# Softmax attention into a soft mixture of experts and a Mish block: the first head pair in an order of its own

## The chip, the cores and the metric

One core of a Trainium2 chip runs the whole program. The metric is device time in microseconds (us) of one execution; the kernel before takes 608.54 us (median of three runs, 608.24 to 610.33).

The engines are named as the profile names them: PE is TensorE (PEld its weight loads), DVE VectorE, ACT ScalarE, POOL GpSimd, SP the engine that issues nearly all DMA transfers. Each works through its own queue in order; a transfer is issued by one engine and carried out by the DMA engines.

## The reference

Three parts run one after the other: attention with rotary embeddings (4 batches, 8 heads, 576 positions, 64 per head), a soft mixture of experts, and a Mish block.

```python
def _attn_ref(q, k, v):
    ...
    def rotate(x):
        x1, x2 = (x[..., :half], x[..., half:])
        return np.concatenate([x1 * cos - x2 * sin, x1 * sin + x2 * cos], axis=-1)
    q_rot, k_rot = (rotate(q), rotate(k))
    scores = scale * np.matmul(q_rot, k_rot.transpose(0, 1, 3, 2))
    scores = scores - np.max(scores, axis=-1, keepdims=True)
    attn = np.exp(scores)
    attn = attn / (np.sum(attn, axis=-1, keepdims=True) + 1e-09)
    return np.matmul(attn, v)
```

The experts and the Mish block come after all the attention; the change touches nothing of them.

## The kernel before

The attention works through 16 pairs of heads. A pair's 576 positions are 512 main rows, loaded as four blocks of 128, and 64 rows that remain, loaded for all heads of a batch at once (`load_rem`).

For each pair, q and k are rotated (`rope_pair`, four tensor operations for each of q and k; `rope_rem` for the remaining rows), transposed on PE (`main_pe`, four transposes each; `rem_pe`, one), and split into a high part, rounded to the format fp32r, and the low part that is left (`main_hi` and `rem_hi` on ACT, `main_lo` and `rem_lo` on DVE, into the buffers `parth` and `partl`, one of each). The parts are then copied into stacks whose upper 64 partitions hold one part and whose lower 64 hold the other: `qk_st`, with k's high part above its low part, and `k2_st`, with the two exchanged, so that two products of 128 partitions give all four terms. For every pair but the first the copying is done by DMA (`stack_dma`, 12 transfers a pair); for the first pair before the change it is done by ACT and POOL (`stack_copy`), save two transfers.

Scores come in nine steps for each pair, S0 to S8 (`scores`): S0, S2, S4, S6 are the four row blocks of head 0, S1, S3, S5, S7 those of head 1, S8 the remaining rows of both. Each is a PSUM tile of two banks (pool `ps_s`, two of them); DVE takes the row maximum (M0 to M8, `maxima`), ACT the exponential with its sum (E0 to E8, `expo`). PE transposes the result (T0 to T7, K0, K1, R, Q), ACT or DVE copies it out (t0 to t7, k0, k1), and PE multiplies it with v (A0 to A4, B0 to B4), followed by x, Y, X and further small steps. All other PSUM tiles share the pool `ps_m` (four of one bank). In between, 20 pieces of later weights are converted from a wider format (`ci`, `Ca` on ACT, `Cb` on DVE, `Cs` on POOL, `co`).

The order of all this is one handwritten list, `PLAN`, gone through once for each pair (a period); `name@n` means that the step is done for the pair n periods back (negative: ahead), so G, ga, gd, Hk, hka, hkd, dk, Hq, hqa, hqd, dq feed the following pair. `keep_in_program_order` holds each engine to it. For the first period the tables `moved` and `shifted` put some steps elsewhere: the feeding of pair 1 begins at S4, pair 1's q is rotated on DVE (`ropeq1`, after M3), and two conversions are begun.

Ahead of the first period stands a prologue: constants and loads on SP, memsets, the rotation of the first k, of the remaining rows of two heads, and of the first q on DVE, the transposes with products of zeros between them (`busy(n)`, n products whose result nobody reads), and the split and the stacking.

Of the kernel before, what the change touches and what calls it, by code (L numbers as in the profile page):

```python
# [35 lines left out]


EVAC = {'t0': 'a', 't1': 'a', 't2': 'a', 't3': 'a', 't4': 'a', 't5': 'd', 't6': 'a', 't7': 'd', 'k0': 'a', 'k1': 'a'}


@with_exitstack
def kernel(
# [28 lines left out]
    psx = ExitStack()  # L71
    ps_s = psx.enter_context(tc.tile_pool(name="ps_s", bufs=2, space=PSUM))
    ps_m = psx.enter_context(tc.tile_pool(name="ps_m", bufs=4, space=PSUM))

# [135 lines left out]

    def load_pair(p, which="qk"):
        b, h = divmod(2 * p, H)
        for nm in which:
            src = q if nm == "q" else k
            t = work(2, 2 * "qk".index(nm) + p % 2, (2, 256))
            dma(out=t, in_=src[b, h:h + 2, 0:512, :].rearrange("h (p c) d -> p h (c d)", c=4))
            raw[nm, p] = t
# [9 lines left out]

    def load_rem(b):
        t = work(1, 3, (H, D))
        dma(out=t[0:R], in_=q[b, :, 512:S, :].rearrange("h s d -> s h d"))  # L230
        dma(out=t[R:128], in_=k[b, :, 512:S, :].rearrange("h s d -> s h d"))
        rem_raw[b] = t

# [42 lines left out]
    def parts_of_pair(p):  # L276
        for x in "hl":
            part[x, p] = ae.tile([128, 2, 640], F32R, tag="part" + x, name="part" + x)
# [21 lines left out]

    def main_part(p, nm, x):
        return part[x, p + 1][:, "qk".index(nm), R:R + 512]

# [79 lines left out]
    def out_of(on, dst, src):  # L383
        (act.copy if on == "a" else dve.tensor_copy)(dst, src)

    def t_copy(p, i):
        t, h = divmod(i, 2)
        tt = t % 2
        out_of(EVAC[f"t{i}"], pt_of(p, t // 2)[:, 5 * h:5 * h + 4, tt * 128:(tt + 1) * 128], m_ps.pop(("T", p, i)))

# [271 lines left out]

    nc.scalar.preload_act_table_set("exp_and_friends")
    pool_.memset(c_all, 0.0)
    dma(out=cs[:, C_COS:C_END], in_=cst[:, C_COS:C_END])
    load_pair(0, "k")
    dma(out=cs[:, 0:C_COS], in_=cst[:, 0:C_COS])
    load_rem(0)
    load_pair(0, "q")
    for i in range(2):  # L670
        dve.memset(qk_st[i][:, QZ:QAR].bitcast(F32), 0.0)
        dve.memset(vrem[i], 0.0)
        dve.memset(zs[i], 1e-9)
    dve.memset(st2, 1e-9)
    dve.memset(tmps[1], 0.0)
    pool_.memset(phi_sb, 0.0)
    load_pair(1, "kq")
    load_vrem(0)
    load_v(0)

    def busy(n):

        ps = ps_m.tile([128, 128], F32, tag="m", name="busy")
        z = c_all[:, 0, 0:4].rearrange("p t s -> p (t s)")
        for _ in range(n):
            pe.matmul(ps, lhsT=z, rhs=z, start=True, stop=True)

    rope_pair(0, "k", dve, ws[0])
    rope_rem(0, dve, 0, 2)
    rope_pair(0, "q", dve, ws[1])  # L690
    busy(14)
    main_pe(-1, "k")
    rem_pe(-1)
    busy(9)
    main_pe(-1, "q")
    busy(12)
    parts_of_pair(0)
    main_hi(-1, "k")
    rem_hi(-1)
    stack_copy(act.copy, "k", 0, "h")  # L700
    stack_copy(act.copy, "k", 1, "h")
    rem_lo(-1)
    main_lo(-1, "k")
    stack_copy(pool_.tensor_copy, "k", 0, "l")
    stack_dma(0, "k", 1, "l")
    main_hi(-1, "q")
    stack_copy(act.copy, "q", 0, "h")
    main_lo(-1, "q")
    stack_copy(pool_.tensor_copy, "q", 0, "l")
    stack_copy(act.copy, "q", 1, "h")  # L710
    stack_copy(act.copy, "q", 1, "l")
    load_v(1)
    for i in range(2):
        dma(out=phi_sb[64 * i:64 * i + 64, :, i], in_=phi.rearrange("(c h p) s -> h p c s", h=2, p=64)[i])
    rope_pair(1, "k", pool_)
    rope_rem(0, pool_, 2, 4)
    load_pair(2)
    load_v(2)
    turns = [(p, k) for p in range(NP) for k in range(2) if not k or p % 2 == 0][:NFB * KDM + NCE]

# [82 lines left out]
    def latest(*steps):  # L803
# [8 lines left out]
    LAST_V = latest(("B4", NP - 2), ("G", NP - 2), LAST_EARLY)  # L812
    moved = {(-1, n) for n in ("G", "ga", "gd", "Hk")}
    moved |= {(0, n) for n in ("hka", "hkd", "dk", "Hq", "hqa", "hqd", "dq", "ropek", "ropeq")}
    steps["ropeq1"] = lambda p: rope_pair(1, "q", dve, ws[1])
    moved |= {(-1, "ld")}
    shifted = {(0, "M3"): [("ropeq1", 0), ("ld", 1)],
               (0, "S4"): [(n, 0) for n in ("G", "ga", "gd", "Hk", "hka", "hkd", "dk")] + [("ropek", 1)],
               (0, "S6"): [(n, 0) for n in ("Hq", "hqa", "hqd", "dq")] + [("ropeq", 1)]}
    for period in range(first, NP + last):  # L820
        for name, n in plan:
            p = period - n
            if period == 0 and p < 0 and name[0] in "TRKB":
                busy(1)
            if 0 <= p < NP and (period, name) not in moved:
                steps[name](p)
                after(name, p)
            for name, p in shifted.get((period, name), ()):
                steps[name](p)
    b = NB - 1  # L830
# [422 lines left out]
```

## Time and profile before

| | us |
|---|---|
| median of three runs | 608.54 |
| the profiled execution, its own time | 609.64 |
| its span, first to last instruction | 607.9 |
| PE busy in it | 588.2 (97%) |
| DVE, ACT, POOL busy in it | 384.1, 341.5, 213.9 |
| scores of pair 0 begin | 14.51 |
| scores of pair 1 begin | 33.48 |
| scores of pair 2 begin | 52.25 |
| scores of pair 3 begin | 70.22 |

Times in the rows below count from the start of the span. In a row of the timeline the first number is the start, the second the duration, then engine, line and operation with what it writes and reads; in brackets stands how long the engine was idle before and what released it. Almost all rows name line 83, which is the helper that keeps the order, so operations are told apart by their tiles: `s` scores, `nmax` maxima, `P` exponentials, `t` and `tk` transposes, `m_k`, `m_q`, `m_rem` the transposed k, q and remaining rows, `m_av` the product with v, `busy` the products of zeros, `w`, `cvw` work areas.

### The profile page before, as it was taken

The page shows a single profiled execution, that of the slowest core. Times are in us where ns is not written, and L with a number is a line of the kernel's source. Part 1 is how long each engine was busy: PE and PEld are TensorE (multiplying, and loading weights), DVE is VectorE, ACT ScalarE, POOL GpSimd, SP SyncE. Part 2 cuts the span into 40 slices and gives each one's busy share as a digit, 9 for nine tenths or more (in the row PEclk, how much of TensorE's full clock was granted, in tenths as well). Part 3 has the DMA queues.
Part 4 walks back from the last instruction along what each step waited for, and adds up shares of the span by engine and source line. Part 5 has one row for each costly group of instructions (what it writes and reads, how often), then busy time and mean ns, then how long its engine had stood idle before and what let it go on. Part 6 is the DMA issues. An engine that isn't in the chain of part 4 may idle for free.

```text
span 607.9 us, 11291 instructions
## 1 busy us (share of the span) xinstructions
PE 588.2 (97%) x4110; PEld 467.0 (77%) x4110; DVE 384.1 (63%) x808; ACT 341.5 (56%) x778; POOL 213.9 (35%) x258
## 2 busy tenths in 40 slices
PE   8899999999999999999998989999999999999996
PEld 8688887878888787787875435777788888888885
DVE  5878887977888777887654332887865333433332
ACT  5787887967889687886761022767662111222211
POOL 2979777587677877673000100000000000000000
PEclk9999999999999999999998999999999999999999
DMA  6897789989999989869869599424003000210004
GB/s 173 233 260 213 208 229 267 252 230 263 262 254 260 256 255 275 228 167 312 245 214 379 196 380 402 173 88 156 11 20 85 0 1 1 66 38 0 2 1 105
DMA packets 59288, 108.82 MB, mean 179 GB/s; under 512 B 12768, under 2 KB 25184, under 8 KB 58720
## 3 DMA queue, kind: packets, MB, share of 16 engines
q1 hardware_dynamic: 59232, 108.09, 60.1%
q8 instruction: 33, 0.54, 0.4%
q14 instruction: 23, 0.19, 0.1%
HBM read 70.25 MB, written 9.96 MB: 132 GB/s over the span
## 4 chain that ended last, share of the span: by engine, by line
PE 80%; DMA 6%; DVE 3%; ACT 2%; issue 1%; SPq 0%; ACTq 0%; DVEq 0%
PE o_ps L1137 32%; PE s L83 12%; PE m_av L83 10%; PE t L83 7%; DMA qk_st<-parth 4%; PE hp L1103 3%; PE h_ps L933 2%; PE so_ps L999 2%; PE m_lg L83 2%; PE warm L557 2%; DMA qk_st<-partl 1%; PE m_x L83 1%; PE m_q L83 1%; ACT P L83 1%; PE m_si L83 1%; PE tk L83 1%
## 5 line engine op out<-in xcount | busy, mean ns | idle before, releaser
L83 DVE TENSOR_REDUCE nmax<-s 128x1 f32<-128x576 f32 x144 | 106.8, 751 | 27.1 <-PE s L83 25.6
L83 ACT ACTIVATE P<-s,nmax 128x576 f32<-128x576 f32 x144 | 107.1, 744 | 18.3 <-DVE nmax L83 17.4
L1137 PE MATMUL o_ps<-wo_l,gh 128*128 128x512 f32 x288 | 112.9, 392 | 0.0
L1137 PE MATMUL o_ps<-wo_h,gh 128*128 128x512 f32 x288 | 112.9, 392 | 0.0
L83 PE MATMUL s<-qk_st 128*128 128x288 f32 x320 | 102.5, 337 | 5.3 <-ACT P L83 4.9
L1110 ACT ACTIVATE room<-hp 128x512 f32<-128x512 f32 x72 | 43.0, 599 | 106.6 <-PE hp L1103 102.0
L1137 PE MATMUL o_ps<-wo_h,gl 128*128 128x512 f32 x288 | 100.6, 390 | 1.0 <-DVE gl L1118 1.0
L83 PE MATMUL s<-k_st,qk_st 128*128 128x288 f32 x320 | 89.2, 295 | 0.0
L83 POOL TENSOR_TENSOR w<-w,cs 128x512 f32<-128x512 f32 (+2 forms) x74 | 86.5, 1190 | 0.9
L83 PE MATMUL t<-cs,P 128*128 128x128 f32 x576 | 83.9, 273 | 0.4 <-ACT P L83 0.4
L83 PEld LDWEIGHTS s<-qk_st 128*128 128x128 f32 x320 | 60.2, 188 | 21.5 <-ACT P L83 9.7
L83 POOL TENSOR_TENSOR w<-w 128x256 f32<-128x256 f32 (+2 forms) x86 | 65.7, 785 | 17.4 <-ACT P L83 14.8
L1112 DVE CAST gh<-room 128x512 fp32r<-128x512 f32 x49 | 20.9, 427 | 79.4 <-ACT room L1110 79.2
L83 PEld LDWEIGHTS t<-cs,P 128*128 128x128 f32 x576 | 68.2, 142 | 0.9 <-ACT P L83 0.7
L83 ACT COPY PT<-t 128x512 f32<-128x512 f32 (+1 forms) x112 | 61.3, 558 | 10.4 <-PE t L83 9.6
L1137 PEld LDWEIGHTS o_ps<-wo_h,gl 128*128 128x128 f32 x288 | 53.9, 188 | 13.3 <-DVE gl L1118 1.7
L1137 PEld LDWEIGHTS o_ps<-wo_h,gh 128*128 128x128 f32 x288 | 54.1, 188 | 9.3
L1137 PEld LDWEIGHTS o_ps<-wo_l,gh 128*128 128x128 f32 x288 | 54.3, 189 | 8.9 <-DVE wo_l L990 0.2
L83 PEld LDWEIGHTS s<-k_st,qk_st 128*128 128x128 f32 x320 | 60.6, 189 | 0.0
L1118 DVE TENSOR_TENSOR gl<-room,gh 128x512 fp32r<-128x512 f32 x72 | 49.6, 690 | 4.6
L83 PE MATMUL m_av<-PT,w 128*64 128x320 f32 (+1 forms) x384 | 52.0, 411 | 0.0
L83 POOL TENSOR_TENSOR c_all<-c_all,tmp 128x64 f32<-128x64 f32 (+1 forms) x44 | 20.9, 474 | 57.6 <-DVE tmp L83 55.8
(154 smaller groups left out, 853.9 us busy)
## 6 DMA issues: line engine op xcount, KB each, us to landing
w<-in_moe_w_dram SPq DMA_DIRECT2D x28, 1024.0 KB, 8.2
w<-in_moe_w_in_dram SPq DMA_DIRECT2D x16, 512.0 KB, 5.4
qk_st<-parth SPq DMA_DIRECT2D x45, 144.0 KB, 5.5
qk_st<-partl SPq DMA_DIRECT2D x45, 144.0 KB, 5.8
room<-in_moe_w_out_dram SPq DMA_DIRECT2D x12, 512.0 KB, 3.5
w<-in_k_dram SPq DMA_DIRECT2D x16, 256.0 KB, 4.1
w<-in_q_dram SPq DMA_DIRECT2D x16, 256.0 KB, 3.9
w<-in_moe_w_dram SPq DMA_DIRECT2D x16, 256.0 KB, 5.4
```

Source lines behind the costliest of these rows:

```text
L83: return lambda *a, **k: tc.keep_in_program_order(f(*a, **k))
L557: tc.keep_in_program_order(nc.tensor.matmul(ps, lhsT=ident, rhs=ident, start=True, stop=True))
L933: nc.tensor.matmul(h_ps[32 * g:32 * g + 32, fh, :], lhsT=si_t[:, c, 32 * e:32 * e + 32], rhs=parts[1, e, hf][0][:, cc * F1 + fh * 512:cc * ...
L999: nc.tensor.matmul(so_ps[32 * g:32 * g + 32, :], lhsT=h_t[eg][:, c, 32 * g:32 * g + 32], rhs=parts[2, e, hf][0][:, cc * DM:(cc + 1) * DM], ...
L1103: pin(nc.tensor.matmul(hp[:, x, :], lhsT=wst[:, f * 128:(f + 1) * 128], rhs=ct[:, i * 256:(i + 1) * 256], start=True, stop=True))
L1110: pin(nc.scalar.activation(out=gg, in_=hp, func=AF.Mish))
L1112: pin((nc.scalar.copy if 0 < u < NG * GR else nc.vector.tensor_copy)(gh, gg))
L1118: pin(nc.vector.tensor_tensor(out=gl, in0=gg, in1=gh.bitcast(F32), op=ALU.subtract))
L1137: pin(nc.tensor.matmul(ops[i, n], lhsT=g_[:, cols], rhs=w_[f], start=(j == 0 and (x, k) == (0, 0)), stop=(j == NG - 1 and all(y[0] != n fo ...
```

## The change

A list `PLAN0` of its own orders the first period; the tables `moved` and `shifted` go. The first pair has three score tiles and two small PSUM tiles instead of two and four; from the second period on the pools are as before. The first k is loaded through ACT's queue, ahead of ACT's table load; the first q is loaded before the remaining rows, and of these two heads first. The rotated first k and q lie in the room of a weight part that is not yet loaded.

The products of zeros go from 44 to 14 (10 before the first transposes, 4 after k's), and none is left in the first period. Head 0's main rows are brought by products with the identity (`twice`) into both halves of a PSUM tile, so that ACT and DVE write high and low parts straight into the stacks, without `stack_copy`; the first 128 columns of q go ahead of the other 384. Head 1 goes the way of all other pairs, with six `stack_dma` transfers. The remaining rows of the first two heads are rotated on POOL, and so is pair 1's q.

In the first period all steps of head 0 up to S6 come first. It converts one piece of weights instead of two (the other goes to pair 1), and feeds pair 2 (G, ga, gd, Hk) only at the beginning of the second period.

```diff
@@ -32,6 +32,13 @@
...
+PLAN0 = (
+    "S4 E0 M2 Hk E2 M4 hka S6 E4 M6 T0 hkd G E6 t0 S1 ga gd dk S3 T2 M1 E1 M3 S5 t2 T1 E3 M5 "
+    "S7 t1 K0 E5 M7 S8 k0 T4 ci1 Hq E7 M8 t4 hqa E8 T3 hqd dq ld:1 ropek:1 t3 A0 z0 ropeR:1 A1 A2 A3 A4 "
+    "ropeq:1 x0 T5 ld:2 Y0 y0 t5"
 ).split()
 
 
...
-    ps_s = psx.enter_context(tc.tile_pool(name="ps_s", bufs=2, space=PSUM))
-    ps_m = psx.enter_context(tc.tile_pool(name="ps_m", bufs=4, space=PSUM))
+    ps_s = psx.enter_context(tc.tile_pool(name="ps_s0", bufs=3, space=PSUM))
+    ps_m = psx.enter_context(tc.tile_pool(name="ps_m0", bufs=2, space=PSUM))
...
-    def load_rem(b):
-        t = work(1, 3, (H, D))
-        dma(out=t[0:R], in_=q[b, :, 512:S, :].rearrange("h s d -> s h d"))
-        dma(out=t[R:128], in_=k[b, :, 512:S, :].rearrange("h s d -> s h d"))
-        rem_raw[b] = t
+    def load_rem(b, h0=0, h1=H):
+        t = rem_raw[b] = work(1, 3, (H, D))
+        dma(out=t[0:R, h0:h1], in_=q[b, h0:h1, 512:S, :].rearrange("h s d -> s h d"))
+        dma(out=t[R:128, h0:h1], in_=k[b, h0:h1, 512:S, :].rearrange("h s d -> s h d"))
...
-        out_of(EVAC[f"t{i}"], pt_of(p, t // 2)[:, 5 * h:5 * h + 4, tt * 128:(tt + 1) * 128], m_ps.pop(("T", p, i)))
+        out_of("d" if p == 0 and i in (1, 3) else EVAC[f"t{i}"], pt_of(p, t // 2)[:, 5 * h:5 * h + 4, tt * 128:(tt + 1) * 128], m_ps.pop(("T", p, i)))
...
-    nc.scalar.preload_act_table_set("exp_and_friends")
     pool_.memset(c_all, 0.0)
     dma(out=cs[:, C_COS:C_END], in_=cst[:, C_COS:C_END])
-    load_pair(0, "k")
+    load_pair(0, "k", act.dma_start)
     dma(out=cs[:, 0:C_COS], in_=cst[:, 0:C_COS])
-    load_rem(0)
     load_pair(0, "q")
+    load_rem(0, 0, 2)
+    nc.scalar.preload_act_table_set("exp_and_friends")
...
+    load_rem(0, 2, H)
     load_vrem(0)
     load_v(0)
 
+
+    st, s2 = qk_st[0], k2_st[0]
+    up, dn = slice(0, 64), slice(64, 128)
+    xk, xq = (ps_s.tile([128, 2, 512], F32, tag="s", name="x" + n) for n in "kq")
+    own = parts[ahead[0]][0]
+    qt, kt = (own[:, o:o + 512].rearrange("p (c x) -> p c x", c=4) for o in (0, 512))
+    scr, scr2 = (own[:, o:o + 512].bitcast(F32R) for o in (1024, 1536))
+    none = ps_m.tile([128, 128], F32, tag="m", name="busy")
+
     def busy(n):
 
-        ps = ps_m.tile([128, 128], F32, tag="m", name="busy")
         z = c_all[:, 0, 0:4].rearrange("p t s -> p (t s)")
         for _ in range(n):
-            pe.matmul(ps, lhsT=z, rhs=z, start=True, stop=True)
-
+            pe.matmul(none, lhsT=z, rhs=z, start=True, stop=True)
+
+    def first(nm, t, tb):
+        rotate(raw.pop((nm, 0)), bc(cs[:, C_COS:C_COS + 256], 2), bc(cs[:, C_SIN:C_SIN + 256], 2),
+               t.rearrange("p c (h d) -> p h c d", h=2), 2, 256, dve, tb)
+
+    def twice(out, t):
+        for half in (up, dn):
+            pe.matmul(out[half], lhsT=t, rhs=ident, start=True, stop=True)
+
+    def lo(out, ps, hi, scale=1.0):
+        dve.scalar_tensor_tensor(out=out, in0=ps, scalar=scale, in1=hi.bitcast(F32), op0=ALU.mult, op1=ALU.subtract)
+
+    def q_hi(o, n):
+        for out, half in ((qm, up), (scr, dn)):
+            act.activation(out=out[half, o:o + n], in_=xq[half, 0, o:o + n], func=AF.Copy, scale=SCALE)
+
+    def q_lo(o, n):
+        lo(qm[dn, o:o + n], xq[dn, 0, o:o + n], scr[dn, o:o + n], SCALE)
+
+    first("k", kt, ws[0])
+    rope_rem(0, pool_, 0, 2)
+    first("q", qt, ws[1])
+    rope["k", 0], rope["q", 0] = kt, qt
+    busy(10)
+    for c in range(4):
+        twice(xk[:, 0, c * 128:(c + 1) * 128], kt[:, c, 0:64])
     main_pe(-1, "k")
+    parts_of_pair(0)
+    hi_, lo_ = part["h", 0], part["l", 0]
+    km, k2m, qm = st[:, KC:KC + 512], s2[:, 0:512], st[:, QA:QA + 512]
+    kr, k2r, qr = st[:, KC + 512:KC + S], s2[:, 512:S], st[:, QAR:QA]
+    act.copy(km[up], xk[up, 0])
+    act.copy(k2m[dn], xk[dn, 0])
+    act.copy(hi_[dn, 1, R:R + 512], m_ps["k", -1][dn])
+    busy(4)
+    twice(xq[:, 0, 0:128], qt[:, 0, 0:64])
+    xr = xq[:, 1]
+    twice(xr[:, 0:128], rem[0][:, 0:64])
+    for c in range(1, 4):
+        twice(xq[:, 0, c * 128:(c + 1) * 128], qt[:, c, 0:64])
+    pe.transpose(xr[:, 128:256], rem[0][:, 0:128], ident)
     main_pe(-1, "q")
+    q_hi(0, 128)
+    lo(k2m[up], xk[up, 0], km[up])
+    lo(km[dn], xk[dn, 0], k2m[dn])
+    q_lo(0, 128)
+    act.copy(kr[up], xr[up, R:128])
+    act.copy(k2r[dn], xr[dn, R:128])
+    lo(k2r[up], xr[up, R:128], kr[up])
+    lo(kr[dn], xr[dn, R:128], k2r[dn])
+    q_hi(128, 384)
+    q_lo(128, 384)
+    xb = xr[dn, 128:256].rearrange("p (a o r) -> p a o r", a=2, o=1).to_broadcast([64, 2, 2, R])
+    hr, lr = (t[dn].rearrange("p a (o r) -> p a o r", r=R)[:, :, 0:10:9, :] for t in (hi_, lo_))
+    act.copy(hr, xb)
+    act.activation(out=hi_[dn, 0, R:R + 512], in_=m_ps["q", -1][dn], func=AF.Copy, scale=SCALE)
+    lo(lo_[dn, 1, R:R + 512], m_ps.pop(("k", -1))[dn], hi_[dn, 1, R:R + 512])
+    dve.tensor_tensor(out=lr, in0=xb, in1=hr.bitcast(F32), op=ALU.subtract)
+    scores(0, 0)
+    scores(0, 2)
+    maxima(0, 0)
+    lo(lo_[dn, 0, R:R + 512], m_ps.pop(("q", -1))[dn], hi_[dn, 0, R:R + 512], SCALE)
+    act.copy(qr[up], xr[up, 0:R])
+    act.copy(scr2[dn, 0:R], xr[dn, 0:R])
+    lo(qr[dn], xr[dn, 0:R], scr2[dn, 0:R])
+    for nm in "kq":
+        for x in "hl":
+            stack_dma(0, nm, 1, x)
...
+    load_v(1)
     rope_pair(1, "k", pool_)
     rope_rem(0, pool_, 2, 4)
+    rope_pair(1, "q", pool_)
     load_pair(2)
     load_v(2)
-    turns = [(p, k) for p in range(NP) for k in range(2) if not k or p % 2 == 0][:NFB * KDM + NCE]
+    turns = [(p, k) for p in range(NP) for k in range(2) if (k if not p else not k or p % 2 == 0 or p == 1)][:NFB * KDM + NCE]
...
-    moved = {(-1, n) for n in ("G", "ga", "gd", "Hk")}
-    moved |= {(0, n) for n in ("hka", "hkd", "dk", "Hq", "hqa", "hqd", "dq", "ropek", "ropeq")}
-    steps["ropeq1"] = lambda p: rope_pair(1, "q", dve, ws[1])
-    moved |= {(-1, "ld")}
-    shifted = {(0, "M3"): [("ropeq1", 0), ("ld", 1)],
-               (0, "S4"): [(n, 0) for n in ("G", "ga", "gd", "Hk", "hka", "hkd", "dk")] + [("ropek", 1)],
-               (0, "S6"): [(n, 0) for n in ("Hq", "hqa", "hqd", "dq")] + [("ropeq", 1)]}
-    for period in range(first, NP + last):
+    begin = [((w + ":0").split(":")[0], int((w + ":0").split(":")[1])) for w in PLAN0]
+    late_feed = [(n, 1) for n in ("G", "ga", "gd", "Hk")]
+    for name, p in begin:
+        steps[name](p)
+    psx.close()
+    ps_s = psx.enter_context(tc.tile_pool(name="ps_s", bufs=2, space=PSUM, reuse_waits="tile"))
+    ps_m = psx.enter_context(tc.tile_pool(name="ps_m", bufs=4, space=PSUM, reuse_waits="tile"))
+    for period in range(1, NP + last):
         for name, n in plan:
             p = period - n
-            if period == 0 and p < 0 and name[0] in "TRKB":
-                busy(1)
-            if 0 <= p < NP and (period, name) not in moved:
+            if (period, name) == (1, "ropek"):
+                for f, i in late_feed:
+                    steps[f](i)
+            if 0 <= p < NP and (name, p) not in begin:
                 steps[name](p)
                 after(name, p)
-            for name, p in shifted.get((period, name), ()):
-                steps[name](p)
```

## Rows read from the trace of the kernel before

**Rows 1.** Stretch, its us; busy PE, PEld, DVE, ACT, POOL; granted clock; DMA share, GB/s.

```profile
0.00:14.51 14.51, 11.90 (x80) 11.48 (x80) 7.93 (x23) 7.07 (x11) 3.06 (x9) 1.00 0.68 172
14.51:33.48 18.97, 16.01 (x122) 13.72 (x123) 13.99 (x22) 12.90 (x30) 18.24 (x21) 1.00 0.88 230
33.48:52.25 18.77, 18.35 (x148) 15.13 (x147) 16.90 (x35) 15.45 (x38) 14.40 (x16) 1.00 0.91 244
52.25:70.22 17.97, 17.97 (x149) 15.10 (x147) 14.10 (x31) 14.39 (x36) 14.11 (x18) 1.00 0.86 224
70.22:88.20 17.98, 17.98 (x148) 15.11 (x147) 15.41 (x34) 15.41 (x38) 14.69 (x17) 1.00 0.76 204
```

**Rows 2.** Timeline, TensorE before the first scores (start, duration, instruction, idle and releaser).

```profile
1.42 6.00 PE L83 MATMUL busy<-c_all 128*128 128x128 f32 x28 [1.42 <-POOL c_all L83]
...
7.26 0.60 PE L83 MATMUL m_k<-cs,w 128*128 128x128 f32 x4
...
14.51 0.40 PE L83 MATMUL s<-qk_st 128*128 128x288 f32 x1 [0.26 <-POOL qk_st L83]
```

**Rows 3.** Timeline, the first loads and the rotations on DVE.

```profile
0.73 0.40 SPq L83 DMA_DIRECT2D cs<-in_constants_dram  x1
...
1.19 0.42 SPq L83 DMA_DIRECT2D w<-in_k_dram  x1
...
4.48 1.29 DVE L83 TENSOR_TENSOR w<-w,cs 128x512 f32<-128x512 f32 x2 [2.12 <-DMA w<-in_k_dram]
...
7.84 0.49 DVE L83 TENSOR_TENSOR w<-w,cs 128x128 f32<-128x128 f32 x2 [1.27 <-DMA w<-in_k_dram]
...
9.97 0.76 DVE L83 TENSOR_TENSOR w<-w,cvw 128x256 f32<-128x256 f32 x2
```

**Rows 4.** Timeline, splitting the first pair into high and low parts.

```profile
9.15 0.37 ACT L83 CAST parth<-m_rem 128x256 fp32r<-128x256 f32 x1 [0.66 <-PE m_rem L83]
...
10.98 0.68 DVE L83 SCALAR_TENSOR_TENSOR partl<-m_k,parth 128x512 fp32r<-128x512 f32 x1
...
12.40 0.60 ACT L83 ACTIVATE parth<-m_q 128x512 fp32r<-128x512 f32 x1
```

**Rows 5.** Timeline, the first pair from its first row maxima on.

```profile
14.54 2.52 POOL L83 TENSOR_TENSOR w<-w,cs 128x512 f32<-128x512 f32 x2
...
15.35 1.52 DVE L83 TENSOR_REDUCE nmax<-s 128x1 f32<-128x576 f32 x2 [1.62 <-PE s L83]
...
16.14 0.74 ACT L83 ACTIVATE P<-s,nmax 128x576 f32<-128x576 f32 x1 [1.05 <-DVE nmax L83]
...
19.30 0.76 DVE L83 TENSOR_TENSOR cvw<-w,cs 128x512 f32<-128x512 f32 x1
...
20.82 1.30 DVE L83 TENSOR_TENSOR w<-w,cvw 128x256 f32<-128x256 f32 x2
...
24.39 0.91 DVE L83 TENSOR_SCALAR w<-w 128x512 uint32<-128x512 uint32 x1
...
25.29 0.40 PE L83 MATMUL s<-qk_st 128*128 128x288 f32 x1 [1.23 <-ACT P L83]
...
27.02 0.83 DVE L83 TENSOR_SCALAR w<-w 128x512 uint32<-128x512 uint32 x1
...
28.83 1.95 PE L83 MATMUL m_av<-PT,v 128*64 128x256 f32 x16
```

**Rows 6.** A transfer issued before 16 us (KB, us to landing); a wait in the timeline.

```profile
qk_st<-partl SPq DMA_DIRECT2D x1, 160.0 KB, 2.5
...
32.30 0.37 ACT L83 CAST parth<-m_rem 128x256 fp32r<-128x256 f32 x1 [0.64 <-DMA qk_st<-parth]
```

**Rows 7.** Stretch, its us; busy PE; granted clock; DMA share, GB/s.

```profile
23.99:27.40 3.41, 1.96 (x15) 1.00 0.95 225
...
323.70:327.80 4.10, 2.39 (x18) 1.00 1.05 407
327.80:331.20 3.40, 3.40 (x19) 0.50 1.05 361
```

More of the change, by code (lines that the diff above doesn't have):

```diff
@@ L34 @@
     "S8 ld@-2 gd@-1 T5 E7 M8 Y0 Hk@-1 "
+).split()
+PLAN0 = (
+    "S4 E0 M2 Hk E2 M4 hka S6 E4 M6 T0 hkd G E6 t0 S1 ga gd dk S3 T2 M1 E1 M3 S5 t2 T1 E3 M5 "
+    "S7 t1 K0 E5 M7 S8 k0 T4 ci1 Hq E7 M8 t4 hqa E8 T3 hqd dq ld:1 ropek:1 t3 A0 z0 ropeR:1 A1 A2 A3 A4 "
+    "ropeq:1 x0 T5 ld:2 Y0 y0 t5"
 ).split()
@@ L209, with load_pair @@
     xg = {}
-    def load_pair(p, which="qk"):
+    def load_pair(p, which="qk", dma=dma):
         b, h = divmod(2 * p, H)
@@ L301, in main_part @@
     def main_part(p, nm, x):
+        if (x, p + 1) not in part:
+            parts_of_pair(p + 1)
         return part[x, p + 1][:, "qk".index(nm), R:R + 512]
@@ L684, in busy @@
         z = c_all[:, 0, 0:4].rearrange("p t s -> p (t s)")
         for _ in range(n):
-            pe.matmul(ps, lhsT=z, rhs=z, start=True, stop=True)
[L688 to L691, printed above, removed]
-    main_pe(-1, "k")
-    rem_pe(-1)
-    busy(9)
-    main_pe(-1, "q")
[L696 to L712, printed above, removed]
+            pe.matmul(none, lhsT=z, rhs=z, start=True, stop=True)
+    def first(nm, t, tb):
+        rotate(raw.pop((nm, 0)), bc(cs[:, C_COS:C_COS + 256], 2), bc(cs[:, C_SIN:C_SIN + 256], 2),
+               t.rearrange("p c (h d) -> p h c d", h=2), 2, 256, dve, tb)
```

## The prediction

> **What bounds the kernel now.** I read the table of stretches first, cut where the scores of pairs 0 to 4 begin. The reader should look for the stretch in which an engine is busy all the time. From the third pair on that is TensorE: 17.97 of 17.97 us and 17.98 of 17.98, while DVE, ACT and POOL have 2.5 to 4 us to spare [rows 1]. A stretch like this can only be moved as a whole. The first two are different: 14.51 us pass before the first scores, and the first pair takes 18.97 us with TensorE busy 16.01 of it, products of zeros included [rows 1]. The change acts here alone, so the sum is this: when do the scores of pair 2 begin (52.25 now)? What follows should move with it.
>
> The timeline before 14.51 shows a chain, and TensorE's share of it is mostly filling: the first 28 passes are products of zeros and end at 7.42 [rows 2]. The chain is: k lands, DVE rotates it from 4.48, DVE then waits 1.27 us for the remaining rows, and finishes q only at 9.97 + 0.76 = 10.73 [rows 3]. ACT, done with the remaining rows' high part at 9.52, makes four copies into the stacks before it reaches q at 12.40 [rows 4]. POOL's copy of q's low part releases S0 [rows 2].
>
> In the first pair the timeline shows DVE as the late one. Pair 1's q is rotated on it from 19.30 to 22.12, and a conversion runs from 24.39 to 27.85 between maxima; the scores at 25.29 then waited 1.23 us for an exponential [rows 5].
>
> **The start, step by step.** k's issue moves from 1.19 to ACT's queue, which can begin with SP's first issue at 0.73 [rows 3]: 0.46 us at best, nothing at worst, since the two loads then compete. I take 4.1 for the first rotation. No load goes through ACT before the change, so the trace can't show it. The Trainium skill (DMA: Bandwidth & Descriptors, Issuing engines are not separate DMA queues) says that transfers issued by ACT and SP run on the same 16 DMA engines and interleave, so that a second issuer saves issue time alone. By that the 0.4 shrinks towards 0, and the time below would be 605.2 in place of 604.8.
>
> k's rotation takes 2.09 as now (4.48 to 6.57) and ends at 6.2. q's load moves up to third on SP; k needed 3.3 us from issue to use [rows 3], so q is there by about 5.3 and is rotated at once: the wait of 1.27 and the remaining rows' rotation (7.84 to 8.65) leave DVE's queue. POOL does that rotation meanwhile. The last two operations of a rotation take 0.76 alone, but 1.30 in the one that runs beside POOL [rows 3, 5]; POOL is busy here, so I take the longer and q is done at 8.8 (8.2 alone).
>
> TensorE's filling ends at 1.42 + 20 × 0.214 = 5.7, before k is ready. The doubled transposes of k are 16 passes with half the columns as weights. Four plain transposes take 0.60 with their tail [rows 2], some 0.11 each, so a pass costs between half of that and all of it: 0.9 to 1.8, twice as much if the clock is still low. ACT's two copies (0.60 each by [rows 4]) end by 9.0. Then DVE has the last word: two low parts of 0.68, three small ones of at most 0.42 [rows 4], some 0.25 by their size: 8.8 + 1.3 + 0.75 = 10.9. The small ones wait for short ACT pieces (0.37 for 256 columns [rows 4]), which run beside the 0.68s. All ends good it is 10.3, all bad 11.5. **S0 at 10.9: 3.6 earlier (3.0 to 4.2).** The four ACT copies and POOL's leave the path altogether.
>
> **The first pair.** Gone from DVE: q of pair 1 (2.8) and the conversion (3.5) [rows 5]. What comes instead:
> S4 needs the tile that holds the raw q, and before that is free DVE does q's 384 columns and two low parts (0.68 each at most), one of 0.42, M0 (0.76) and a small one: S4 at S0 + 3.4. S2 has run, TensorE waits about 1.7.
> G stands before S1 and needs one of the two small tiles, which hkd frees: S1 at S0 + 6.7. The six transfers for head 1 start at S0 + 0.8; the last is issued near S0 + 4 and lands 2.5 later [rows 6], so it ends no wait here, unless it is as slow as one for which ACT waited 0.64 us until 32.30 [rows 6].
> gd stands before M1 on DVE and waits for ga, which stands behind E6 and t0 on ACT: E1 at S0 + 9.0, about 1.2 lost, with E3, E5, E7, E8 behind it.
> ACT from E0 (S0 + 2.7): nine exponentials at 0.76 (0.74 and a step [rows 5]), five copies of 0.5 to 0.6 and two of 0.37 [rows 4]: 10.4, and with that wait and the smaller ones the end of E8 is at S0 + 15.
> Behind hqa come hqd and t3 on DVE (0.68 each), then A: 20 passes at 1.95 / 16 = 0.12 [rows 5], x0 (0.37) and Y0 (0.4). **The next S0 at S0 + 18.9 (17.5 to 20.4), against 18.97.** The order trades the old waits for new ones.
> POOL: busy 18.24 of 18.97 now [rows 1], and pair 1's q adds 3.8 (2.52 for its two large operations, half that for the two of half the size). But its queue starts near 6 in place of 14.54 [rows 5]: k of pair 1 is ready by 12, remaining rows by 14, q by 18, where Hk, G and Hq want them at 14.8, 17.4 and 24. Hidden by 2.8 us or more; without that cover each us late is a us lost, as Hk holds TensorE's queue.
>
> **The second pair** takes 18.77 now, 0.8 above the 17.97 of the next [rows 1]. The old pair's E8 and t5 are already done, which takes some of the 0.8; G and Hk of pair 2 are added, five transposes, 0.55. I take 18.7 (18.5 to 19.1). The conversion moved to the third period costs nothing: the fourth has two and takes 17.98 against 17.97, its DVE and ACT at 15.4 [rows 1].
>
> **Sum.** Pair 2's scores begin at 10.9 + 18.9 + 18.7 = 48.5 in place of 52.25: 3.75 less. The profiled execution took 609.64, with 1.7 outside its span of 607.9; it would take 605.9. The median is 1.1 below the profiled one: 608.54 - 3.75 = **604.8**.
>
> **Rivals.** *The clock falls for a while.* 30 of 44 products of zeros go, all within the first pair among them. In the tail of the attention TensorE was busy 2.39 of 4.10 us and then ran at a granted 0.50, 1.2 GHz, from 327.8 to 331.2; in the first pair it was busy 1.96 of 3.41 and stayed at 1.00 [rows 7]. By the steps above the changed kernel is near 1.1 of 3.4 between S0 and S4, lower than either. For it: that. Against: such a hole may fall on two sides. Work at half speed on the path, some 0.8 to 2.0 us each time: 605.6 to 607.3. The Trainium skill (TensorE: Matmul & The Clock Gate, What's actually happening) says that "the default state is throttled, and activity releases the throttle"; the fall in rows 7 agrees.
> *The small tiles bind.* Two instead of four, so a transpose waits for the copy before last. If each of the four waits (G, T1, T4, T3) costs 0.5 to 1 more than I have, and transfers land in 3.3 and more: 606.8 to 608.5. For it: the list crosses engines at each step; against: ACT has the same waits covered.
> *It starts no earlier.* k and q land no sooner, or the doubled passes cost the upper bound at the low clock: S0 at 12.5 or later, 606.5 to 608.3.
> *Slower: the clock stays low throughout.* Filling ends at 5.7 and holes follow; if the rise (the filling's 0.214 a pass becomes 0.11 near 7 us, [rows 2]) doesn't come before the second pair, the first pair's TensorE work, some 11.5 us (16.01 less the filling, pair 2's transposes and the modelled tails), doubles to 23 and passes the pair's 18.9 by 4, and its place on the path adds 3 and the start 3: 611 to 615. It decides once more than about 4 us of TensorE's work on the path run at half speed.
>
> **How the numbers follow.** Forecast 0.54 (602.9 to 606); clock falls for a while 0.22; small tiles 0.12; no earlier start 0.06; slower 0.06. 0.5%, about what a measurement of this kernel can tell from no change, is 3.0 us, so 605.5 is the border: nine tenths of the forecast's case and a quarter of the next lie below it: faster 0.54; slower 0.07 with a little from the tiles' tail; the rest 0.39. Range 602.9 (both first terms at their good ends) to 608.3 (the end of the third case).
>
> **What would show it.** The first S0 near 10.9, the first q rotation ending near 8.8 without a wait for a load; S4 3.4 after S0; S1 released by hkd's tile or by a transfer; pair 1's S0 near 29.8, pair 2's near 48.5, then pairs of 18.0 as before. A granted clock of 0.50 between 10 and 30 would be the first rival. I am wrong if later pairs grow: then the stages behind weren't bound by TensorE alone.

## The result, and the profile of the changed kernel

The changed kernel is slower: 614.69 us median (612.87 to 620.71, 13 runs) against 608.24 for the kernel before (13 runs), a ratio of 1.0113, 95% interval 1.0078 to 1.0148. Forecast were 604.8 us and a range up to 608.3. The profiled execution took 613.82 us, with a span of 612.0.

The table of stretches again has a cut where each pair's first scores begin (columns as in [rows 1]); the last row is the stretch at the low clock, which lies inside the second.

```profile
0.00:11.97 11.97, 8.60 (x74) 7.69 (x74) 7.57 (x19) 3.50 (x7) 6.14 (x12) 1.00 0.67 181
11.97:37.31 25.34, 16.71 (x99) 12.99 (x100) 13.46 (x25) 13.07 (x34) 17.02 (x23) 0.87 0.78 187
37.31:56.15 18.84, 18.84 (x150) 15.65 (x151) 15.83 (x33) 15.23 (x37) 13.27 (x14) 1.00 1.06 260
56.15:74.13 17.98, 17.98 (x148) 15.11 (x147) 15.80 (x34) 15.41 (x38) 16.86 (x20) 1.00 0.86 235
74.13:92.22 18.09, 18.09 (x149) 15.14 (x147) 15.36 (x34) 15.38 (x38) 15.52 (x17) 1.00 0.76 205
15.00:21.80 6.80, 4.49 (x19) 3.74 (x17) 4.29 (x8) 2.45 (x7) 4.13 (x5) 0.50 0.74 150
```

In these executions the start gained 2.5 us (11.97 for 14.51), the first pair lost 6.4 (25.34 for 18.97), and the pairs behind it take what they took [rows 1]. The second pair's first scores begin at 37.31 instead of 33.48, and the 3.8 us stay: the last scores are 5.8 late, the span 4.1 longer. In 25.34 us TensorE is busy 16.71, and DVE and ACT 13: nothing there is full, so the stretch is a chain of waits. The list that follows the chain back from the second pair's first scores (start, us, what) names it:

```profile
16.76 0.59 SPq L90
...
17.45 1.29 DMA qk_st<-parth
18.74 3.07 issue
...
21.89 0.60 ACT parth L90
...
24.71 0.42 DVE partl L90
25.14 0.68 DVE nmax L90
...
30.28 0.61 ACT parth L90
...
31.64 5.54 DMA qk_st<-partl
37.17 0.14 issue
37.31 0.77 PE s L90 x4
```

Both ends are stacking transfers: at 17.45 one for head 1 of the first pair, behind which ACT's `parth` at 21.89 (this is hka) stands, and at 31.64 one for the second pair's q, which the scores at 37.31 wait for. The timeline of ACT, PE and SP between (start, duration, instruction, idle and releaser):

```profile
21.89 0.60 ACT L90 ACTIVATE parth<-m_k 128x512 fp32r<-128x512 f32 x1 [3.15 <-PE t L90]
...
23.36 0.31 PE L90 MATMUL m_rem<-cs,w 128*128 128x128 f32 x1 [2.16 <-DVE partl L90]
23.59 0.37 PE L90 MATMUL s<-qk_st 128*128 128x288 f32 x1
...
37.31 0.37 PE L90 MATMUL s<-qk_st 128*128 128x288 f32 x1 [1.55 <-DMA qk_st<-partl]
...
14.91 0.53 SPq L90 DMA_DIRECT2D qk_st<-parth  x1
...
18.09 0.57 SPq L90 DMA_DIRECT2D qk_st<-partl  x1
18.75 2.08 SPq L90 DMA_DIRECT2D phi_sb<-in_moe_phi_dram  x2
...
22.04 0.47 SPq L90 DMA_DIRECT2D w<-in_k_dram  x1
```

The first row is a trap. It puts 3.15 us of hka's wait down to the transposes `t`, and these had long been done (20.14 to 21.2). Hka writes a new tile in the one room of `parth`, which three of the six transfers still read; the last of those three landed at 21.74. G (23.36) needs the tile that hkd frees, and S1 (23.59) stands behind G. SP meanwhile reaches phi, v and the third pair's q and k only behind the six, at 18.75 to 22.6.

### The profile page after: what moved, and what is told of

Read it like the earlier page. It is cut to its first block, busy times and chain, and to the rows that moved or that the text cites. A ratio compares the mean times of both kernels' runs of the same rounds, so it can differ in the third digit from the quotient of the medians.

```text
span 612.0 us, 11260 instructions
## 1 busy us (share of the span) xinstructions
PE 584.5 (96%) x4086; PEld 461.7 (75%) x4086; DVE 384.2 (63%) x809; ACT 338.9 (55%) x779; POOL 218.2 (36%) x263
## 4 chain that ended last, share of the span: by engine, by line
PE 86%; DMA 5%; DVE 3%; ACT 3%; issue 1%; SPq 1%; DVEq 0%; ACTq 0%
PE o_ps L1197 32%; PE s L90 13%; PE m_av L90 12%; PE t L90 9%; DMA qk_st<-partl 3%; PE hp L1163 3%; PE h_ps L993 2%; PE so_ps L1059 2%; PE m_lg L90 2%; DMA qk_st<-parth 2%; PE m_x L90 1%; PE warm L565 1%; PE m_q L90 1%; PE tk L90 1%; PE m_k L90 1%
## 5 line engine op out<-in xcount | busy, mean ns | idle before, releaser
L90 ACT ACTIVATE P<-s,nmax 128x576 f32<-128x576 f32 x144 | 107.1, 745 | 17.9 <-DVE nmax L90 16.8
L90 POOL TENSOR_TENSOR w<-w,cs 128x512 f32<-128x512 f32 (+2 forms) x78 | 90.6, 1182 | 16.1 <-DMA w<-in_k_dram 15.2
L90 POOL TENSOR_TENSOR w<-w 128x256 f32<-128x256 f32 (+2 forms) x88 | 67.1, 782 | 14.8 <-ACT P L90 11.7
```

The costliest lines, as they stand in the source:

```text
L90: return lambda *a, **k: tc.keep_in_program_order(f(*a, **k))
```

## The experiments

"hka" is the splitting of the second pair's k, "second pair" its first scores, "low" the time at a granted clock of 0.50 in the first pair; all in us, from the profiled execution. The ratio is the time over that of the kernel before on the same chip.

| kernel | S0 | hka | S1 | second pair | low | ratio (95%) |
|---|---|---|---|---|---|---|
| before | 14.5 | 21.8 | 15.3 | 33.5 | 0 | 1 |
| changed | 12.0 | 21.9 | 23.6 | 37.3 | 6.8 | 1.0113 (1.0078 to 1.0148) |
| e1_parts | 11.8 | 19.3 | 22.2 | 37.7 | 10.2 | 1.0114 (1.0050 to 1.0177) |
| e2_fill | 11.8 | 21.8 | 23.6 | 37.2 | 0 | 1.0111 (1.0052 to 1.0172) |
| e4_before_few | 13.5 | 22.0 | 14.7 | 36.1 | 12.1 | 1.0021 (0.9995 to 1.0047) |
| e7_copies | 13.6 | 24.7 | 27.3 | 39.9 | 13.7 | 1.0115 (1.0068 to 1.0161) |
| e9_order_alone | 13.5 | 18.4 | 20.5 | 33.6 | 6.8 | 1.0003 (0.9973 to 1.0033) |
| e11_pool_behind | 12.0 | 19.5 | 22.8 | 35.1 | 10.2 | 1.0043 (1.0003 to 1.0083) |
| e12_early | 12.7 | 20.2 | 23.4 | 36.9 | 10.2 | 1.0079 (1.0042 to 1.0117) |
| e14_front | 11.9 | 17.1 | 19.4 | 31.0 | 0 | 1.0006 (0.9978 to 1.0033) |
| e15_front_nofill | 12.0 | 16.4 | 20.2 | 32.1 | 6.8 | 1.0004 (0.9971 to 1.0037) |
| e17_front_bank | 12.2 | 16.8 | 19.6 | 31.0 | 0 | 0.9996 (0.9959 to 1.0032) |
| e18_order_only | 12.2 | 17.0 | 21.8 | 37.4 | 9.2 | 1.0102 (1.0067 to 1.0138) |
| e19_loads_first | 12.3 | 16.4 | 22.0 | 34.7 | 10.2 | 1.0055 (1.0021 to 1.0089) |

**Room, clock, products of zeros.** The first theories were A, the room of `parth` holds hka, and B, the clock.

```diff
# e1_parts: pair 0's parts in spare rooms
-    parts_of_pair(0)
+    for i, x in enumerate("hl"):
+        part[x, 0] = parts[ahead[1 + i]][0][:, 0:1280]...
# e2_fill: 6 products of zeros behind S2, 8 behind T0
+    fill(2, 6)
...
+        if name == "T0": fill(6, 8)
# e4_before_few: the kernel before with the change's 10 + 4 products
-    busy(14)   -    busy(9)   -    busy(12)   -    busy(1), in period 0
+    busy(10)   +    busy(4)
```

> The changed kernel, with the high and low parts of pair 0 in two rooms of weight parts not yet loaded, so that pair 1's parts need not wait until the transfers of head 1 have read the only parth and partl. Theory A (the queue: ACT stood from 18.7 to 21.9 before pair 1's high part because of those transfers, and DVE, G and S1 stood behind it): the wait goes, pair 1's scores begin near 34 in place of 37.31, and the time falls by about 3 us, to 611 or 612. Theory B (the clock: TensorE ran at 1.2 GHz from 15.0 to 21.8 and that set the first pair's length): the hole between S2 and S4 is still there, so the clock falls as before; pair 1 begins within 1 us of 37.3 and the time stays within 1 us.

> The changed kernel with products of zeros put back into the two holes of the first pair: 6 after S2 and 8 after T0, into unused columns of score tiles. Theory B (the clock): the granted clock stays at 1.00 through the first pair, pair 1 begins 2 to 4 us earlier (33.5 to 35.5) and the time falls as much. Theory A (the queue): the clock stays high, but ACT still waits for the transfers until about 21.8, so pair 1 begins within 0.7 us of 37.3 and the time falls by 0.7 us at most.

> The kernel before with the changed kernel's number of products of zeros: 10 before the first transposes, 4 behind k's, none in the first pair; nothing else is changed. Theory B (the clock): the granted clock falls in the first 35 us here too, and the time rises by 2 to 6 us. Theory A (the queue): the time stays within 1 us of the kernel before, as the old order has TensorE waiting less.

Stretch of the first pair in e1_parts, then in e2_fill:

```profile
11.80:37.69 25.89, 18.14 (x100) 14.87 (x100) 13.65 (x25) 13.44 (x34) 16.09 (x22) 0.80 0.79 186
```

```profile
11.83:37.16 25.33, 18.18 (x128) 14.55 (x128) 13.47 (x25) 13.06 (x34) 16.75 (x22) 1.00 0.78 185
```

and in e1_parts hka and the second pair's first scores:

```profile
19.25 0.60 ACT L90 ACTIVATE parth<-m_k 128x512 fp32r<-128x512 f32 x1 [0.68 <-PE m_k L90]
...
37.69 0.37 PE L90 MATMUL s<-qk_st 128*128 128x288 f32 x1 [2.69 <-DMA qk_st<-partl]
```

Both theories fall as the whole cause. In e1_parts hka comes 2.6 us earlier, so the room did hold it; but the second pair starts no earlier: its scores then wait 2.69 us for a transfer of its own q. In e2_fill the clock stays at 1.00 through the first pair, which takes 25.33 us. Both together, with the 6 products behind S2 alone (e3_parts_fill), gave 24.69, with two stretches of 3.4 us at the low clock, and a ratio of 1.0119. In e4_before_few the fewer products cost the old order 3.6 us in the first pair, with the clock low from 11.9 to 25.6 (the second pair is 2.7 later, as S0 came 1.0 earlier; the time is not clear of that of the kernel before). So the clock has a price where TensorE is on the path, and in the changed kernel it isn't.

**Start or order?** Head 1 stacked by engine copies instead of transfers, and the new order behind the old start:

```diff
# e7_copies
     for nm in "kq":
-        for x in "hl":
-            stack_dma(0, nm, 1, x)
+        stack_copy(act.copy, nm, 1, "h")
+        stack_copy(pool_.tensor_copy, nm, 1, "l")
# e9_order_alone: the old prologue, then
+    scores(0, 0); scores(0, 2); maxima(0, 0)
+    for name, p in begin: ...                     # PLAN0, three score tiles, two small tiles
```

> The changed kernel, but head 1 of the first pair is stacked by six engine copies (three on ACT, three on POOL) instead of six transfers. Theory C (transfers): the transfers that landed at 21.7 to 22.1 us held hka and S1 back; with copies hka starts by 19.5 us, S1 by 21.5 (it was 23.6), and the first pair takes 22.5 to 23.5 us instead of 25.3: 611 to 612.5 us. Theory D (the order itself): with two small PSUM tiles the chain hka, hkd, G, ga, S1 stays as long, the first pair stays at 24.5 us or more and the time at 613 to 615.

> The kernel before up to its first scores (its start, its stacks, its zero products), then the changed kernel's order for the first pair with its three score tiles and two small tiles; q of the second pair rotated on POOL as in the change. Theory C: head 1's operands are in place within 1 us of the first scores, so the new order has nothing to wait for: first scores at 14.5 us, first pair 18.5 to 20 us, 608 to 609.5 us. Theory D: the order itself is too long, the first pair takes 22.5 us or more, 612 us or more.

POOL's timeline in e7_copies:

```profile
17.15 0.71 POOL L90 CAST qk_st<-partl 64x640 fp32r<-64x640 f32 x1 [7.62 <-DVE partl L90]
...
19.43 2.49 POOL L90 TENSOR_TENSOR w<-w,cs 128x512 f32<-128x512 f32 x2
```

e7_copies missed by my own doing: I had put POOL's copies ahead of the second pair's rotation, so POOL stood 7.62 us for a low part and the rotation of k began at 19.43 instead of 9.6; hka went to 24.7. It says nothing about transfers. (e8_copies_ci, which also issued the 512 KB load later, and e10_start_alone, the same start under the old order, had the same fault: first pairs of 26.3, ratios of 1.0107 and 1.0126. In e10_start_alone S1, second in the old order, also waited 4.42 us for ACT's copies of head 1.) e9_order_alone is the clear one: from where the operands are ready, the new order takes 20.06 us, 1.1 more than the old one, and the time is that of the kernel before. The first pair of e9_order_alone, and TensorE's wait there for the second pair's k:

```profile
13.55:33.61 20.06, 16.25 (x103) 13.65 (x101) 9.88 (x16) 11.29 (x27) 19.17 (x24) 0.83 0.74 185
```

```profile
17.63 0.66 PE L90 MATMUL m_k<-cs,w 128*128 128x128 f32 x4 [2.24 <-POOL w L90]
```

The 1.1 us hold 6.8 us at the low clock and this wait of 2.24 for POOL's rotation, which no run takes apart. So in this execution the order with what comes with it costs 1.1 us, and by itself perhaps nothing; the rest is what the start leaves behind, head 1 above all. Two more things can be read off this run. Behind the old start S2 and S4 begin at 14.18 and 14.70, in the change at 14.54 and 17.23: of these steps the new start brings forward S0 alone. And S0 is at 13.55 here and at 14.51 in the profile of the kernel before, with the same instructions ahead of it, so a gain in S0 read from two executions is good to about 1 us.

**Without the six transfers.** The copies go to POOL alone, behind its rotations, high parts first; then the splitting of k also moves forward:

```diff
# e11_pool_behind: without the six stack_dma, and
     rope_pair(1, "k", pool_)
     rope_rem(0, pool_, 2, 4)
+    for x in "hl":
+        for nm in "kq":
+            stack_copy(pool_.tensor_copy, nm, 1, x)
     rope_pair(1, "q", pool_)
# e15_front_nofill: this, e1_parts' rooms, k loaded by SP, and
-    "S4 E0 M2 Hk E2 M4 hka S6 E4 M6 T0 hkd G E6 t0 S1 ga gd dk S3 ... T4 ci1 Hq
+    "ci1 Hk S4 hka E0 M2 hkd E2 G M4 S6 ga E4 M6 T0 gd E6 t0 S1 dk S3 ... T4 Hq
# e14_front: e15_front_nofill and e2_fill's 6 products behind S2
```

> The changed kernel, but head 1 of the first pair is stacked by six copies on POOL, placed behind POOL's rotation of k and of the remaining rows of the second pair (and before its q), high parts first, so that neither a transfer nor a waiting POOL holds hka. Theory E (all runs so far: the second pair's first scores start 15.2 to 15.4 us after hka, the splitting of its k, wherever that lies): hka at 18.7 to 19.5 us instead of 21.9, second pair's first scores at 34.0 to 35.0 us instead of 37.3, 611 to 612.5 us. If the transfers were not what held hka, it stays at 21 us or later and the time at 614 us or more.

> The changed kernel with five edits: first pair's split parts in rooms of their own, head 1 stacked by six POOL copies behind the second pair's rotations, the transposes of the second pair's k ahead of S4 and their splitting ahead of the first exponential, the conversion's 512 KB load issued ahead of all stack transfers, k of the first pair loaded by SP; and six zero products behind the third scores. If the late splitting and S1 are the rest of the loss (a): hka by 17.5 us, S1 at 20 to 21 us, second pair's first scores 11.3 to 12.5 us behind S1, at 31.5 to 33.5 us, and 606.5 to 609 us, level with the kernel before or a little below. If the start or the clock are the rest, they stay at 34.5 us or later and the time at 611 us or more.

> As e14_front without the six zero products. If the clock matters (c), the granted clock is low for 6 to 14 us in the first pair and its second pair's first scores start 0.8 to 2 us later than in e14_front; if it doesn't, within 0.5 us.

First pair and second pair in e14_front:

```profile
11.86:30.99 19.13, 16.01 (x111) 12.57 (x112) 12.54 (x23) 12.83 (x34) 18.01 (x25) 1.00 0.69 183
30.99:50.27 19.28, 18.84 (x152) 15.61 (x152) 17.08 (x35) 15.24 (x37) 16.28 (x18) 1.00 0.90 240
```

and the first pair in e15_front_nofill:

```profile
11.98:32.10 20.12, 16.86 (x99) 13.56 (x100) 12.64 (x23) 13.28 (x34) 19.00 (x26) 0.83 0.67 173
```

Without the transfers, and with the change's own list, 2.2 us come back (e11_pool_behind); with the splitting moved forward, and the rooms, the conversion's load and k on SP beside it, the second pair starts at 32.1, 5.2 earlier than in the change, and with the clock kept up at 31.0, 6.3 earlier and 2.5 before the kernel before. (e12_early moved hka but left the transposes that it reads behind S4 on TensorE, where they ended only at 20.15; e13_all added further edits to that, and its eight products behind T0 held M6, which reads the same tile: DVE stood 3.20 us before it, and the ratio was 1.0124. Both missed.)

**What the six transfers do.** e18_order_only has the moved order with the transfers back; e19_loads_first also puts the loads of phi, v, and the third pair's q and k ahead of them on SP.

```diff
# e18_order_only: e15_front_nofill with the six stack_dma(0, nm, 1, x) and k on ACT's queue
# e19_loads_first: e18_order_only, with the transfers moved down to here
     load_pair(2)
     load_v(2)
+    for nm in "kq":
+        for x in "hl":
+            stack_dma(0, nm, 1, x)
```

> The changed kernel with e15_front_nofill's order and rooms, but with the six transfers for head 1 and k on ACT's queue, as in the change. If S1 hangs on the transfers once hka no longer does: hka at 16 to 17.5 us, S1 at 22 to 23 us when the last of them has landed, second pair's first scores 11.3 to 12.5 us behind it, at 33.5 to 35 us: 610.5 to 613 us, so that order and transfers each give about half. If the early splitting alone sets the end, the second pair starts at 31.5 to 32.5 us as in e15_front_nofill and the time is 609 to 610.5 us.

> As e18_order_only, but the loads of phi, of v for the second and third pair and of the third pair's q and k stand ahead of the six transfers on SP's queue. If the loads behind the six transfers held the second pair: they are issued from 9 to 12 us instead of 19.0 to 22.7, POOL no longer waits for the third pair's k, the second pair's stack transfers land within 3 us of issue, and its first scores start at 32.5 to 34 us instead of 37.4: 609.5 to 612 us. If only the six transfers themselves count, S1 stays at 21.5 to 22 us and the second pair's first scores at 36 us or later, 614 us or more.

Transfers issued between 23.2 and 27.8 us in e18_order_only (KB, us to landing), TensorE's waits for S1 and for the second pair there, and SP's own waits between 20 and 38 us (in total, times, longest):

```profile
qk_st<-parth SPq DMA_DIRECT2D x1, 160.0 KB, 8.3
...
qk_st<-partl SPq DMA_DIRECT2D x1, 144.0 KB, 9.2
k_st<-partl SPq DMA_DIRECT2D x1, 144.0 KB, 8.8
```

```profile
21.76 0.37 PE L90 MATMUL s<-qk_st 128*128 128x288 f32 x1 [0.96 <-ACT P L90]
...
37.39 0.58 PE L90 MATMUL s<-qk_st 128*128 128x288 f32 x1 [4.11 <-DMA qk_st<-partl]
```

```profile
SPq L90 <- DMA w<-in_moe_w_in_dram: 2.4, 1, 2.4
SPq L90 <- DMA w<-in_v_dram: 1.3, 1, 1.3
```

and the same transfers, issued between 19.8 and 25.6, with S1's wait, in e19_loads_first (`w` is the spare room that now holds the first pair's parts):

```profile
qk_st<-parth SPq DMA_DIRECT2D x1, 160.0 KB, 6.1
...
qk_st<-partl SPq DMA_DIRECT2D x1, 144.0 KB, 5.6
k_st<-partl SPq DMA_DIRECT2D x1, 144.0 KB, 5.7
```

```profile
21.96 0.58 PE L90 MATMUL s<-qk_st 128*128 128x288 f32 x1 [1.05 <-DMA qk_st<-w]
```

So the six transfers hold the second pair in three ways. They hold hka by the room (e1_parts frees it). They hold S1 by its operands: in e19_loads_first the row names the transfer, and S1 is at 22.0, against 20.2 with copies. (In e18_order_only S1 is at 21.8; there the last of the six, landed at 21.56, and an exponential that ended at 21.51 can't be told apart.) And, standing first on SP's queue until 18.7, they hold the loads behind them, which then stand just ahead of the second pair's own transfers: those take 8 to 9 us to land in e18_order_only.

How that makes TensorE wait 4.11 us, the rows of SP show. In all 19 traces SP's transfers land in the order of their issue, and never are more than eight in flight. In e18_order_only SP stood 1.3 us until a load of v had landed (29.08) and 2.4 until the conversion's load had (31.92); it issued q's first transfer at 32.63, although q's high part was done at 28.40. The moved order has a share in this: it issues the conversion's 512 KB load at 22.70, ahead of the pair's transfers, where the change issues it at 29.80. In e19_loads_first it is ahead of them too (19.08), and SP issues q's first transfer at 30.02, right behind its high part.

Taking away one way shows the next: the second pair starts at 37.3 in the change, at 37.7 with the room freed (e1_parts) and at 37.4 with the splitting moved forward as well (e18_order_only). Loads first gives 2.7 us (e19_loads_first, somewhat later than I had expected, with 10.2 us at the low clock), copies, with k on SP and 6.8 us at the low clock, another 2.6.

**The first block of q.**

```diff
# e16_bank; e17_front_bank is this and e14_front
-    twice(xq[:, 0, 0:128], qt[:, 0, 0:64])
+    twice(xk[:, 1, 0:128], qt[:, 0, 0:64])      # and q_hi, q_lo read it there
```

> The changed kernel, but the first block of q goes to the idle second bank of k's PSUM tile instead of the bank that holds the other three blocks. If the first block gained nothing in the change because its split waited for every product into its tile, ACT's first split of q starts 0.5 to 0.9 us earlier (10.1 to 10.6 us instead of 11.03) and the first scores start at 11.1 to 11.6 us instead of 11.97; the second pair's first scores, which hang on hka, stay at 37 to 37.5 us and the time at 613 to 615 us. If the split is held by something else, it stays at 11.0.

> e14_front and e16_bank together. If the start is still on the path (b), the second pair's first scores start 0.4 to 0.9 us earlier than in e14_front; if S1 hangs on POOL's copies of head 1, they start within 0.3 us of it.

ACT's first splitting of q, in the changed kernel and in e17_front_bank:

```profile
11.03 0.27 ACT L90 ACTIVATE qk_st<-xq 64x128 fp32r<-64x128 f32 x1 [1.33 <-PE xq L90]
```

```profile
9.82 0.27 ACT L90 ACTIVATE qk_st<-xk 64x128 fp32r<-64x128 f32 x1 [0.29 <-PE xk L90]
```

In the other tile the first block is split 1.2 us earlier, so the change had it wait for the products of the other blocks. But S0 starts no earlier (12.16): DVE's low part of k, at 9.19 in e14_front, now waits for ACT's pieces of q, which read the same tile:

```profile
10.42 0.68 DVE L90 SCALAR_TENSOR_TENSOR k_st<-xk,qk_st 64x512 fp32r<-64x512 f32 x1 [1.22 <-ACT w L90]
```

The turns that ACT and DVE take go with the shared tile and only changed their place. S0's second half is 0.3 sooner (12.65 instead of 12.92), and the second pair not at all (30.96 against 30.99): S1 waits 0.24 for POOL's copy. (In e16_bank's profiled execution the clock rose only at 10.4 us and S0 began at 14.0; its two runs settle no time.)

**Where the 2.5 us of e14_front go.** It is 2.0 us ahead at the fourth and fifth pair but level at the last scores (316.3 against 316.1), and its median is that of the kernel before, within an interval of 0.4% to either side; so are e15_front_nofill and e17_front_bank. One giving-back is shown: the second pair takes 19.28 for 18.77, and 20.83 in e17_front_bank, where ACT waits for a conversion's load:

```profile
42.13 1.21 ACT L90 ACTIVATE w<-w 128x512 f32<-128x512 f32 x2 [1.94 <-DMA w<-in_moe_w_in_dram]
```

The rest goes behind the fifth pair's first scores, where the code is the same in all these kernels and one execution still differs from another by 5 us and more; it stays open. The ratios hint at the start: in the eight kernels of the table with the new start and ten runs or more the time is 1.0 to 3.0 us longer than the second pair's shift would make it, in the two with the old start (e4_before_few, e9_order_alone) it is 1.3 us shorter and equal. What that is, no run shows. No version here beats the kernel before beyond what its measurement can tell.

## Why the prediction was wrong, by its own steps

*What bounds the kernel*: right. From the third pair on the stretches take 17.98 and 18.09 with TensorE busy throughout, and what the first pair lost moved what follows: pairs 2 to 4 begin 3.9 to 4.0 us late. Of the 7.65 us between forecast (48.5) and measurement (56.15) for pair 2's scores, 1.1 are in S0, 6.4 in the first pair and 0.1 in the second.

*k's issue on ACT*: the forecast of 4.1 for the first rotation failed; it was 4.75. In the 12 profiled kernels with k on ACT's queue it began at 4.46 to 5.38 (median 4.86); in the 7 with k on SP, the kernel before included, at 4.46 to 4.73 (median 4.56). The Trainium skill (DMA: Bandwidth & Descriptors, Issuing engines are not separate DMA queues) says that the two issuers' transfers interleave on the same DMA engines; these rows agree, and even the saved issue time is not seen.

*Rotations*: q's rotation needed no load, as forecast, took 2.6 us as forecast, and ended at 9.38 instead of 8.8: the 0.6 is k's late start. *Doubled transposes*: within 1.1 us (6.90 to ACT's start at 8.04), at the good end. *The small ones beside the 0.68s* failed: ACT and DVE read one PSUM tile and took turns, with waits of 0.36, 0.50, 0.52 and 1.05 us between 11.3 and 13.9. Some of these are waits for a part that the other has to make first; that the shared tile is enough for one, e17_front_bank showed (1.22). S0 began at 11.97 with one half only; its other half came at 13.02 and S2 at 14.54. The term was 10.9, with 11.5 for "all bad". The first and the last of the four waits:

```profile
11.95 0.20 ACT L90 CAST qk_st<-xq 64x64 fp32r<-64x64 f32 x1 [0.36 <-DVE qk_st L90]
...
13.92 0.56 DVE L90 SCALAR_TENSOR_TENSOR qk_st<-xq,w 64x384 fp32r<-64x384 f32 x1 [1.05 <-ACT w L90]
```

*The first pair, S0 + 18.9*: measured S0 + 25.34. S4 at S0 + 3.4: measured 5.26, the 1.7 us of waiting as forecast but from a later S2. **S1 at S0 + 6.7, and the transfers "end no wait", is the step that failed**: S1 came at S0 + 11.6, because hka, ahead of G and S1 in the chain, stood until 21.89 for the room that the transfers read. I had one transfer's 2.5 us [rows 6] for all six and their issue at S0 + 0.8. They were issued from S0 + 2.9, landed 2.4 to 4.3 us later, the last at S0 + 10.2, and I had not asked what else they hold: the room of the parts, and SP's queue. *E8's end at S0 + 15*: S0 + 19.5. From there to the next scores I had 3.9; it was 5.8, with 1.55 for the second pair's q transfer, the kind of wait that [rows 6] showed at 32.30.

*The order* itself was nearly sized right: 18.9 forecast, 20.06 measured in e9_order_alone, 6.8 of it at the low clock. *POOL hidden*: right for k, remaining rows and q of the second pair (ready at 13.6, 15.2, 19.3); but POOL then stood 7.34 us, to 26.63, for the third pair's k, whose load SP had issued only at 22.04. *Second pair*: 18.84 for 18.7. *The moved conversion*: free (17.98, 18.09).

*Rivals*: the clock did fall, 15.0 to 21.8, but behind the transfers that cost nothing (e2_fill); its price showed once they were gone: 1.1 us in the second pair's start (e15_front_nofill against e14_front), though the two medians are equal (609.72 and 609.71). The small tiles bound nothing beyond the 1.1 of the order. "Starts no earlier" was half true: k landed no sooner, and S0 came early but S2 and S4 didn't. The slower rival had the wrong mechanism; the one that came, transfers on the path, stood in the text only as an aside.

*From 3.8 us to the median*: the profiled execution lost 4.2, the medians differ by 6.4. The mean granted clock of the 13 runs is 0.985 to 0.994, with 0.994 in the profiled one; in 13 runs of the kernel before (beside e1_parts) it is 0.994 to 1.000. What part of the other 2 us that makes, no run separates.

## What to carry to other kernels

When copies by engines become transfers, price three things: when the last of them lands, which buffer they keep from its next writer, and what stands behind them on the issuing queue; each can hide the next, so that removing one may show nothing. In a chain of waits, find an instruction that the end follows at a steady distance (here hka, 15.2 to 15.7 us before the second pair in eight of the sixteen kernels with the new order), ask of each variant when that comes, and where the distance changes (13.9 to 20.4 us in the other eight) look for what bound there instead: a transfer, S1 or the clock. Starting earlier is worth something only if all that the first stage needs comes earlier, not its first operand alone.

## What the runs showed of the hardware that I had not expected

A 144 to 160 KB stacking transfer landed 2.4 us after its issue when little else ran, 5.5 us behind a 512 KB load, and 8.1 to 9.3 us behind that and four loads of 256 KB. No transfer of SP overtook one issued before it in any of the 19 traces (some 380 transfers each), and at most eight were in flight at once; where SP stood for the oldest of eight, it issued the next at once (29.09 behind a landing at 29.08 in e18_order_only).

With the change's start the granted clock rose to 1.00 between 4.3 and 6.8 us in 13 profiled executions and only at 10.4 to 10.7 in three, and then S0 was at 13.6 to 14.0. The Trainium skill (TensorE: Matmul & The Clock Gate, What's actually happening) says that activity releases the throttle; here the same activity did so at two times 4 us apart.

In the 25 runs of the kernel before beside e14_front, time and mean granted clock go together with a correlation of -0.76: 605.69 to 614.31 us in one and the same kernel.
